# Attention and mixture-of-experts kernel: a third expert slot is multiplied by seven products of halves

## Chip, cores and metric

One core of a Trainium2 chip runs the whole kernel in one launch. The metric is the device time of an execution in microseconds; three executions of the kernel before gave 539.89, 539.95 and 541.04 us.

## What is computed

```python
# attention over 32 memories; batch 8, heads 8, seq 576, head_dim 64
a = softmax(phi, axis=memories)
k_m = einsum('bhsm,bhsd->bhmd', a, k); v_m = einsum('bhsm,bhsd->bhmd', a, v)
attn = softmax(q @ k_m^T / 8) @ v_m
x = attn.transpose(0, 2, 1, 3).reshape(4608, 512)
# mixture of 8 experts, one for each token
logits = x @ w_gate                       # 4608 x 8
e_idx = argmax(logits, axis=1)
gate_w = softmax(logits)[e_idx]
eom = sigmoid(x @ w_output_gate)
for e in range(8):
    h  = relu(x[e_idx == e] @ w1[e])      # 512 -> 1024
    out[e_idx == e] = gate_w * eom[:, e] * (h @ w2[e])   # 1024 -> 512
```

## The kernel before

The program has two parts that overlap. The first computes attention and writes x to a DRAM buffer `xs`, two batches ("pair") at a time; VectorE (DVE) then ranks the tokens by expert (`rank`) and derives lists of token rows, an early list from the first two pairs (`route_early`) and a late one when all four are through (`route_late`). A list is made by `table`: DVE compares (line 232, tile `eql`), TensorE (PE) adds up 144 small products (line 242, PSUM tile `pr`), DVE writes the indices.

The second part runs eight big **slots** of 576 tokens of one expert each, slots 0 to 3 from the early list and 4 to 7 from the late one (with these inputs no smaller slot is used after them). For a slot GpSimd (POOL) gathers the rows of x (`gathers`, line 441), they are transposed and cut into a high and a low part (`xh`, `xl`, `turn_x`), and each weight block of 128x1024 (`w`, fetched by SyncE, line 495) is cut likewise by `Stream.split`: ScalarE (ACT) casts the high part (line 537), DVE subtracts for the low one (line 542), into a ring of buffers `whl`. Every product is three matmuls: high by high, low by high, high by low. The first layer gives `hh` and `hl` (lines 1276 and 1281), the second `y` (line 1442), which is scaled and scattered by POOL (line 1267). `nine` emits a slot; its second layer also prepares the next slot's x.

The first layer exists in two forms. `plain` (slots 0, 1, 2, in `WHOLE`) transposes x on PE (lines 1136, 1141) and multiplies whole: 16 banks (PSUM tiles of 288 columns) of 12 matmuls, 192 in all (line 1310). `seven` (slots 3 to 7, in `SEVEN`) splits both operands in halves and forms seven products P1 to P7 of 4 x 6 matmuls, 168 in all (line 1338). It needs sums of weight quarters (S1 to S4, `Stream.prep`: DVE lines 511, 517, 519, POOL line 515), sums of x quarters (T1 to T4, DVE line 1120) and x transposed by DVE instead of PE: `relay` moves squares of 32 rows by 16 DMAs on SyncE's queue (line 457, tile `xq`), line 1102 transposes them. A `seven` slot has 11 splits, a `plain` one 8.

The order of work on each engine is the order in which the program emits it. After each bank a `hook` advances what runs beside the slots: attention by `HOOK[0]` pieces and the ranking by `HOOK[1]` pieces. `LATE` holds a piece back for so many ticks after what it needs was emitted. `SUMS6`, `EXTRA6`, `TURN6`, `GATHER` and `RELAY` say at which steps of a slot the preparation of the next one is emitted; steps 0 to 15 are its first layer, 16 to 35 its second.

Buffers come from stacked pools. `settle` (when attention is done, at the end of slot 0) closes the attention's pools, `reopen` (step 2 of slot 2) closes the ranking's, and each calls `grow(k)`, which adds `GROW[k]` buffers to the rings (`whl`, `w`, `xg`). `rebank` deals the eight PSUM banks anew: 4 for `ps`, 4 for `pc`, which the seven products accumulate in.

Of the kernel before, what the change touches and what calls it, by code (L numbers as in the profile page):

```python
# [7 lines left out]
F32 = mybir.dt.float32  # L8
# [8 lines left out]
P = 128  # L17
B, H, S, D, M = 8, 8, 576, 64, 32
NTOK, DM, E, F = 4608, 512, 8, 1024
# [8 lines left out]
SL = S  # L28
NHB = SL // 64
NCL = (NHB + 1) // 2  # L30
NPE, NPL, NSS = 4, 4, 28
# [4 lines left out]
ORDER = ["R4", "X", "S", "R0", "m", "D", "M", "B", "V0", "R1", "R1", "V1", "M", "W", "m", "C"]  # L36
LAG = {"X": 1, "B": 2, "D": 1, "V": 3, "C": -1}
TICK = 0
HOOK = (3, 2)
START = 17  # L40
SWAP = ()
NKV = 8
# [7 lines left out]
NPK = 1  # L50
PHI1 = 6
NEA = 3
LATE = {"lg": 8, "w": 2, "pe": 3, "dve": 2}
GROW = ((4, 0, 0), (2, 0, 0), (0, 2, 0))
SOON = {"pe": 3, "dve": 0, "tab": 12, "w": 3, "ix": 2}
PACE = 30
BESIDE = ((14, 15), (13, 14))
# [7 lines left out]
EXTRA6 = (1, 3, 11, 14, 17, 19)  # L65
EXTRA7 = (2, 6, 9, 12, 17, 19)
GATHER = {8: 2, 12: 2, 16: 1}
LAST = 1
OPEN = (2, 2)
WHOLE = tuple(range(NPE - 1))  # L70
SEVEN = tuple(range(NPE - 1, NPE + NPL))
PROD = ("P1", "P2", "P6", "P5", "P3", "P7", "P4")
SPLITS = {"P1": (0, 2), "P6": (2,), "P5": (0, 2)}
SUMS = {"P6": "S2", "P5": "S1", "P3": "S4", "P7": "S3"}
FREED = {"P1": 0, "P2": 0, "P6": 0, "P5": 1, "P3": 0, "P7": 2}
XQ = 144
XROW = 4 * XQ


HEADS = (0, 2, 4, 6, 1, 3, 5, 7)  # L80
# [3 lines left out]
def attention_moe(tc, phiT, kv, qT, wgo, wall, out):  # L84
    nc = tc.nc
    V, A, G, T = nc.vector, nc.scalar, nc.gpsimd, nc.tensor

    with contextlib.ExitStack() as ctx:
# [30 lines left out]
        prt = ctx.enter_context(contextlib.ExitStack())  # L119
# [265 lines left out]
        env = {}  # L385
# [36 lines left out]
        ring = Ring([P, 2, 1024], F32R, "whl")  # L422
# [24 lines left out]
        def relay(z, to=4):  # L447

            if not z["quart"]:
                return  # L450
            if "xq" not in z:
                z["xq"] = env["st"].tile([P, NCL, 4, P], F32, name="xq")
                z["a"] = 0
            for a in range(z["a"], to):
                for b in range(4):
                    m = 1 if not z["big"] else NCL if b < 2 else NCL - 1
                    nc.sync.dma_start(z["xq"][32 * a:32 * a + 32, 0:m, b],
                                      z["xg"][32 * b:32 * b + 32, 0:m, XQ * a:XQ * a + P])
                z["a"] = a + 1

# [609 lines left out]
        def turn_x(z, c):  # L1070
# [3 lines left out]
            nb, n = (NCL, SL) if big else (1, P)  # L1074
            if c == 0:
# [6 lines left out]
                m = min(nb, 4)  # L1082
# [17 lines left out]

            def square(c):
                V.transpose(z["xt"][:, c, 0:n].rearrange("p (k i) -> p k i", i=32),
                            z["xq"][:].rearrange("p k b q -> p (k b) q")[:, 0:n // 32, 32 * c:32 * c + 32])

            if z["seven"]:
                xt = z["xt"].rearrange("p a (b s) -> p a b s", b=2)

                src = {"B11": xt[:, 0:2, 0], "B21": xt[:, 2:4, 0], "B22": xt[:, 2:4, 1]}
                if c == 0:
                    for k in range(4):  # L1110
                        square(k)
                elif c == 1:
                    for nm in src:
                        A.copy(z[nm][0], src[nm])
                    tr = env["st"].tile([P, NCL, 4, P], F32, name="xq")[:].rearrange("p k b q -> p (k b q)")
                    z["r"] = r = {nm: tr[:, SL * o:SL * o + SL].rearrange("p (a s) -> p a s", a=2)
                                  for o, nm in enumerate(("T1", "T2", "T3", "T4"))}
                    for nm, x, y in (("T1", xt[:, 0:2, 1], xt[:, 0:2, 0]), ("T2", xt[:, 2:4, 1], r["T1"]),
                                     ("T3", xt[:, 2:4, 1], xt[:, 0:2, 1]), ("T4", xt[:, 2:4, 0], r["T2"])):
                        V.tensor_tensor(r[nm], x, y, ALU.subtract)  # L1120
                elif c == 2:
                    for nm, x in z["r"].items():
                        A.copy(z[nm][0], x)
                    for nm in src:
                        V.tensor_tensor(z[nm][1], src[nm], z[nm][0].bitcast(F32), ALU.subtract)
                else:
                    for nm, x in z["r"].items():
                        V.tensor_tensor(z[nm][1], x, z[nm][0].bitcast(F32), ALU.subtract)
                return
# [115 lines left out]
        mo = None  # L1245
# [9 lines left out]
        PASS = ((0, 0), (1, 0), (0, 1))  # L1255

        def finish_y(z, k, py):
            y = mo.tile([P, DM], F32, name="y", bufs=4)
            n = P
            if k == NCL - 1:  # L1260

                n = 64
                A.copy(y[0:n], py[64:128])
                V.tensor_tensor(y[0:n], py[0:n], y[0:n], ALU.add)
                py = y
            A.activation(y[0:n], py[0:n], AF.Copy, scale=z["g"][0:n, k:k + 1])  # L1266
            G.indirect_dma_start(  # L1267
                out=out, out_offset=bass.IndirectOffsetOnAxis(ap=z["idx"][1][0:n, z["q0"] + k:z["q0"] + k + 1], axis=0),
                in_=y[0:n], in_offset=None, bounds_check=NTOK - 1, oob_is_err=False)
# [47 lines left out]
        def seven(i, st, hook):  # L1317

            z, h = order[i], [hidden() for _ in range(4)]
            if "pad" not in env:  # L1320
                env["pad"] = env["st"].tile([P, 24], F32, name="pad")
            step, made = [-1, 0], [None]

            def tell(new=None):
# [89 lines left out]
        def nine(i, st, nxt, hook):  # L1414

            z = order[i]
            h = (seven if z["seven"] else plain)(i, st, hook)
            wei.finish()
            more = i + 1 < st.hi and order[i + 1]["seven"]
            if more and "pc" not in env:  # L1420
                rebank()
            turn, extra, sums = (TURN, (), {}) if not more else (
                (TURN7, EXTRA7, SUMS7) if z["seven"] else (TURN6, EXTRA6, SUMS6))
            if z["seven"]:
# [90 lines left out]
        def settle():  # L1515

            att.finish()
            pso.close()
            pa.close()
            env["rl"] = prl.enter_context(tc.tile_pool(name="rl", bufs=1, side="right", reuse_waits="tile"))  # L1520
            env["cap"] = raw.size
            grow(1)
            env["ps"] = prp.enter_context(tc.tile_pool(name="p1", bufs=7 - NPK, space=PSUM, reuse_waits="tile"))
# [2 lines left out]

        def reopen():

            late.finish()
            prl.close()  # L1530
            prt.close()
            env["st"] = ctx.enter_context(tc.tile_pool(name="st", bufs=1, side="right", reuse_waits="tile"))
            grow(2)
            env["cap"] = raw.size

        def rebank():
            prp.close()
            prr.close()
            for key, nm, n in (("ps", "p2", 4), ("pc", "pc", 4)):
                env[key] = ctx.enter_context(tc.tile_pool(name=nm, bufs=n, space=PSUM, reuse_waits="tile"))  # L1540

        def run(st):
# [8 lines left out]
            def hook(step, new):  # L1551
                if (i, step) == OPEN:
                    reopen()
                wei.step()
                if step < 16 or not drip.gens:
                    gathers(i)
                if i + 1 < hi and order[i + 1]["seven"]:
                    if step in RELAY and (gat[0] > i + 2 or gat[0] > i + 1 and not drip.gens):
                        relay(order[i + 1], 2 * RELAY.index(step) + 2)
                clock[0] += not att.gens  # L1560
                att.step(HOOK[0])
                (rou if rou.gens else late).step(HOOK[1])

# [25 lines left out]
        n = NPE + NPL  # L1589
# [52 lines left out]
```

## Time and profile before

| | |
|---|---|
| median of 3 executions | 539.95 us (539.89 to 541.04) |
| the profiled execution's own time | 543.56 us |
| its span, first to last instruction | 541.6 us |
| PE busy | 506.0 us (93%) |
| DVE busy | 375.6 us (69%) |
| ACT busy | 280.9 us (52%) |
| POOL busy | 164.8 us (30%) |
| mean granted TensorE clock | 0.964 of full speed |

The profile is of one execution. A matmul's recorded duration overlaps the next one's, so PE is read here by when a stage starts and ends, not by the sum of durations. The slots stand in it as follows (us from the span's start): slot 0 from 118.1, its second layer from 150.4; slot 1 from 183.1, second layer from 209.0; slot 2 from 240.9, second layer from 266.4; slot 3, the first of seven products, from 292.5, second layer from 314.8; slot 4 from 340.95. PE ends at 534.85.

### The profile page before, as it was taken

Reading aid. Unit: us, or ns where it says so; the run is one execution under the profiler, and the core shown is the slowest. Engines: PE = TensorE matmul, PEld = TensorE weight load, DVE = VectorE, ACT = ScalarE, POOL = GpSimd, SP = SyncE. Lnnn points to the kernel's source line nnn. Section 1 sums busy time; section 2 is a strip of 40 time slices with the busy share of each in tenths; the row PEclk is TensorE's granted clock in tenths of the full one; section 3 lists DMA queues with packets and bytes.
Section 4 is the critical chain, followed back from the end, with each engine's and each line's share of the span. In section 5 each row is a group of like instructions: output and inputs, shape, how many; then the busy total and the mean of one; then the engine's idle time right before and its main releaser. Section 6 shows DMA issues by size and latency. Waiting matters only on the chain. (4 is left out here: it accounts for less than half of the span.)

```text
span 541.6 us, 11081 instructions
## 1 busy us (share of the span) xinstructions
PE 506.0 (93%) x4205; PEld 429.5 (79%) x4205; DVE 375.6 (69%) x870; ACT 280.9 (52%) x535; POOL 164.8 (30%) x168
## 2 busy tenths in 40 slices
PE   3788886989999999999999999999999999999995
PEld 2455554769877898789988988998898899889983
DVE  4374889787942698545593898688789878978600
ACT  4475764265533453244264756665574666548311
POOL 2242554543421330214146114302621341130021
PEclk9977998599999999999999999999999999999999
DMA  8999999888353664218407832980594188130011
GB/s 317 424 392 386 413 412 398 289 308 254 128 170 110 213 224 125 88 50 322 87 12 229 268 78 72 304 209 8 178 267 133 45 292 216 36 95 34 0 50 45
DMA packets 42111, 104.01 MB, mean 192 GB/s; under 512 B 4992, under 2 KB 16576, under 8 KB 41664
## 3 DMA queue, kind: packets, MB, share of 16 engines
q1 hardware_dynamic: 36160, 83.15, 46.0%
q0 software_dynamic: 5888, 20.06, 10.8%
q8 instruction: 35, 0.57, 0.4%
q14 instruction: 28, 0.23, 0.1%
HBM read 77.23 MB, written 20.05 MB: 180 GB/s over the span
## 5 line engine op out<-in xcount | busy, mean ns | idle before, releaser
L1442 PE MATMUL bps<-whl,hh 128*128 128x512 f32 x560 | 170.4, 398 | 0.0
L542 DVE TENSOR_TENSOR whl<-w,whl 128x1024 fp32r<-128x1024 f32 x74 | 90.7, 1233 | 48.6 <-ACT whl L537 40.2
L1442 PEld LDWEIGHTS bps<-whl,hh 128*128 128x128 f32 x560 | 104.7, 188 | 24.7
L1442 PE MATMUL bps<-whl,hl 128*128 128x512 f32 x216 | 85.4, 395 | 0.0
L537 ACT CAST whl<-w 128x1024 fp32r<-128x1024 f32 x74 | 76.8, 1049 | 4.3 <-PE bpc L1442 2.8
L1310 PE MATMUL bps<-xh,whl 128*128 128x288 f32 x384 | 77.6, 298 | 0.0
L1310 PEld LDWEIGHTS bps<-xh,whl 128*128 128x128 f32 x384 | 61.5, 188 | 1.3 <-DVE gr L1061 0.4
L1267 POOL DMA_INDIRECT out<-y,idx_oa x20 | 26.0, 1300 | 105.3 <-ACT y L1266 80.9
L1310 PE MATMUL bps<-xl,whl 128*128 128x288 f32 x192 | 54.8, 296 | 0.0
L1267 POOL DMA_INDIRECT out<-y,idx_ol x20 | 22.7, 1137 | 104.0 <-ACT y L1266 70.5
L1338 PE MATMUL bpc<-xh,whl 128*128 128x288 f32 x240 | 49.4, 296 | 0.0
L1338 PE MATMUL bpc<-th,whl 128*128 128x288 f32 x240 | 49.3, 295 | 0.0
L1442 PEld LDWEIGHTS bps<-whl,hl 128*128 128x128 f32 x216 | 40.7, 188 | 9.3
L1266 ACT ACTIVATE y<-bps,gx 128x512 f32<-128x512 f32 x27 | 18.6, 689 | 44.7 <-PE bps L1442 39.8
L1276 ACT ACTIVATE hh<-bps 128x288 fp32r<-128x288 f32 x48 | 19.7, 411 | 39.9 <-PE bps L1310 38.8
L1338 PEld LDWEIGHTS bpc<-xh,whl 128*128 128x128 f32 x240 | 38.9, 188 | 0.2
L1338 PEld LDWEIGHTS bpc<-th,whl 128*128 128x128 f32 x240 | 39.0, 188 | 0.0
L1276 ACT ACTIVATE hh<-keep 128x288 fp32r<-128x288 f32 x60 | 26.7, 445 | 22.7 <-DVE keep L1349 22.7
L901 ACT COPY xo<-bpd 128x576 f32<-128x576 f32 x36 | 22.2, 641 | 28.1 <-issue 9.5
L1310 PEld LDWEIGHTS bps<-xl,whl 128*128 128x128 f32 x192 | 35.6, 188 | 0.2
L857 POOL TENSOR_TENSOR ea<-ea,mx 128x512 f32<-128x512 f32 (+1 forms) x18 | 17.6, 977 | 59.5 <-DVE mx L855 51.3
L1338 PE MATMUL bpc<-tl,whl 128*128 128x288 f32 x120 | 35.4, 295 | 0.0
(246 smaller groups left out, 950.3 us busy)
## 6 DMA issues: line engine op xcount, KB each, us to landing
w<-wall SPq DMA_DIRECT2D x64, 512.0 KB
kvt<-kv SPq DMA_DIRECT2D x32, 512.0 KB
xs<-xo SPq DMA_DIRECT2D x16, 576.0 KB
qt<-qT SPq DMA_DIRECT2D x16, 512.0 KB
ph<-phiT SPq DMA_DIRECT2D x3, 1152.0 KB
xq<-xg SPq DMA_DIRECT2D x40, 80.0 KB
xq<-xg SPq DMA_DIRECT2D x40, 64.0 KB
kv<-kv SPq DMA_DIRECT2D x4, 512.0 KB
```

The source lines that it names most:

```text
L537: A.copy(hl[:, 0], w[:])
L542: V.tensor_tensor(hl[:, 1], w[:], hl[:, 0].bitcast(F32), ALU.subtract)
L857: (V if z["k"] in BESIDE[0] else G).tensor_tensor(eav, eav, mx[:, 0:n].unsqueeze(2).to_broadcast([P, n, M]), ALU.subtract)
L901: A.copy(xo[:, c % 2], px[:, :, 0:2 * XQ])
L1266: A.activation(y[0:n], py[0:n], AF.Copy, scale=z["g"][0:n, k:k + 1])
L1267: G.indirect_dma_start(out=out, out_offset=bass.IndirectOffsetOnAxis(ap=z["idx"][1][0:n, z["q0"] + k:z["q0"] + k + 1], axis=0), in_=y[0:n] ...
L1276: A.activation(h_[:, j, c:e], src, AF.Relu)
L1310: T.matmul(pb, w[:, b, o:o + P], x[a][:, cc, c * SL // 2:(c + 1) * SL // 2], start=(n == 0), stop=(n == 11))
L1338: T.matmul(pb, w[:, b, o:o + P], z[x][a][:, kc], start=(first and n == 0), stop=(n == 5), skip_group_check=not first)
L1442: T.matmul(py, a, w[:, b, DM * f:DM * f + DM], start=(u == 4 and f == 0 and n == 0), stop=(u == 7 and f == 1 and n == len(ps) - 1))
```

## The change

Slot 2 leaves `WHOLE` and joins `SEVEN`. The pool `st`, which holds `xq`, the sums and the kept products, is opened in `settle` rather than in `reopen`, and the ranking's pool `rt` is kept to the end; `xq` loses 2 of 20 blocks, a pad goes, `y` has 3 buffers rather than 4. The rings grow in another order: 6, then 7, then 8 buffers for `whl` (before 6, 8, 8), 5, 6, 7 for `w` (before 5, 5, 7). `rebank` stands at the start of slot 2 rather than before slot 2's second layer. Attention and ranking advance by 4 and 3 pieces a hook rather than 3 and 2, the ranking's PE work is held back 5 ticks rather than 3, and one more split is emitted at step 12 of slot 2 (`MORE`).

```diff
-HOOK = (3, 2)
+HOOK = (4, 3)
-LATE = {"lg": 8, "w": 2, "pe": 3, "dve": 2}
-GROW = ((4, 0, 0), (2, 0, 0), (0, 2, 0))
+LATE = {"lg": 8, "w": 2, "pe": 5, "dve": 2}
+GROW = ((4, 0, 0), (1, 1, 0), (1, 1, 0))
-LAST = 1
+LAST = 0
 OPEN = (2, 2)
-WHOLE = tuple(range(NPE - 1))
-SEVEN = tuple(range(NPE - 1, NPE + NPL))
+MORE = (2, 12)
+WHOLE = tuple(range(NPE - 2))
+SEVEN = tuple(range(NPE - 2, NPE + NPL))
...
-                z["xq"] = env["st"].tile([P, NCL, 4, P], F32, name="xq")
+                z["xq"] = env["st"].tile([P, NXQ, P], F32, name="xq")
...
-                    nc.sync.dma_start(z["xq"][32 * a:32 * a + 32, 0:m, b],
+                    nc.sync.dma_start(z["xq"][32 * a:32 * a + 32, b:4 * m - 3 + b:4],
...
-            y = mo.tile([P, DM], F32, name="y", bufs=4)
+            y = mo.tile([P, DM], F32, name="y", bufs=3)
...
             z = order[i]
+            if z["seven"] and "pc" not in env:
+                late.finish()
+                rebank()
             h = (seven if z["seven"] else plain)(i, st, hook)
             wei.finish()
             more = i + 1 < st.hi and order[i + 1]["seven"]
-            if more and "pc" not in env:
-                rebank()
...
             pa.close()
+            env["st"] = ctx.enter_context(tc.tile_pool(name="st", bufs=1, side="right", reuse_waits="tile"))
...
         def reopen():
-            late.finish()
             prl.close()
-            prt.close()
-            env["st"] = ctx.enter_context(tc.tile_pool(name="st", bufs=1, side="right", reuse_waits="tile"))
             grow(2)
...
             def hook(step, new):
                 if (i, step) == OPEN:
                     reopen()
+                if (i, step) == MORE:
+                    st.split(ring.size, wait=True)
```

In the built program slot 2's 192 matmuls of line 1310 and its 20 transposes are gone and 168 matmuls of line 1338 stand in their place. Lines of the changed kernel are one or two higher than those before (542 is 544, 232 is 234, 1310 is 1312, 1338 stays). Three places in the order of the engines follow.

DVE, before, where the late list is compared: all of it stands in slot 1's second layer, since the row above it finishes a `y`.

```order
L1264 TENSOR_TENSOR y<-bps,y 64x512
L371 TENSOR_TENSOR q_3069<-q_3069,q_3066 128x36
L373 TENSOR_TENSOR q_3063<-q_3063,q_3069 128x36
L215 TENSOR_TENSOR tm<-ohg,tb 128x288
L219 TENSOR_REDUCE q_3104<-tm 128x36
L376 TENSOR_TENSOR q_3104<-jg,q_3104 128x36
L378 TENSOR_TENSOR q_3063<-q_3063,q_3104 128x36
L232 TENSOR_TENSOR eql<-iota_bl,q_3063 128x864 x4
L542 TENSOR_TENSOR whl<-w,whl 128x1024
```

And in the change:

```order
L544 TENSOR_TENSOR whl<-w,whl 128x1024
L1283 SCALAR_TENSOR_TENSOR hl<-bps,hh 128x288
L378 TENSOR_TENSOR q_2940<-jg,q_2940 128x36
L380 TENSOR_TENSOR q_2889<-q_2889,q_2940 128x36
L234 TENSOR_TENSOR eql<-iota_bl,q_2889 128x864
L1283 SCALAR_TENSOR_TENSOR hl<-bps,hh 128x224
L1283 SCALAR_TENSOR_TENSOR hh<-bps,hh 128x64
L234 TENSOR_TENSOR eql<-iota_bl,q_2889 128x864 x3
L1283 SCALAR_TENSOR_TENSOR hl<-bps,hh 128x288
L1283 SCALAR_TENSOR_TENSOR hl<-bps,hh 128x224
L1283 SCALAR_TENSOR_TENSOR hh<-bps,hh 128x64
L544 TENSOR_TENSOR whl<-w,whl 128x1024
```

The comparisons moved up into slot 1's first layer, among the remainders of its banks 8 to 11 of 16 (two halves 288 and 224 + 64 a pair of banks).

PE, before, from the end of the list's 144 products into slot 1's second layer:

```order
L242 LDWEIGHTS Aw
L242 MATMUL pr<-eql,Aw 64x48
L1442 MATMUL bps<-whl,hh 128x512
L1442 MATMUL bps<-whl,hl 128x512
L1442 MATMUL bps<-whl,hh 128x512 x2
L1442 MATMUL bps<-whl,hl 128x512
L1442 MATMUL bps<-whl,hh 128x512
L1136 MATMUL bps<-ident,xg 128x128 x4
L1141 MATMUL bps<-ident,xg 128x64 x4
L1442 MATMUL bps<-whl,hh 128x512
```

And in the change:

```order
L244 LDWEIGHTS Aw
L244 MATMUL pr<-eql,Aw 64x48
L1443 MATMUL bps<-whl,hh 128x512 x17
L1443 MATMUL bps<-whl,hl 128x512
L1443 MATMUL bps<-whl,hh 128x512 x2
L1443 MATMUL bps<-whl,hl 128x512
```

The list's products moved from within the second layer to its very front (the 17 matmuls begin with the 16 of its first row block), and the transposes no longer follow.

SyncE's queue, before, at the fetch of slot 2's weights during slot 1's first layer:

```order
L493 TENSOR_LOAD slot
L493 ISA x2
L495 ISA
L495 DMA w<-wall 128x1024
L495 ISA
L495 DMA w<-wall 128x1024
L495 ISA
L495 DMA w<-wall 128x1024
L495 ISA
L495 DMA w<-wall 128x1024
L495 ISA
L495 DMA w<-wall 128x1024
```

And in the change:

```order
L497 ISA
L497 DMA w<-wall 128x1024
L459 DMA xq<-xg 32x5x128 x2
L459 DMA xq<-xg 32x4x128 x2
L459 DMA xq<-xg 32x5x128 x2
L459 DMA xq<-xg 32x4x128 x2
L497 ISA
L497 DMA w<-wall 128x1024
L459 DMA xq<-xg 32x5x128 x2
L459 DMA xq<-xg 32x4x128 x2
L459 DMA xq<-xg 32x5x128 x2
L459 DMA xq<-xg 32x4x128 x2
```

Sixteen moves for slot 2 now stand in two halves round the fetch of its fifth weight block; the four blocks that its sums need are ahead of them.

## Rows read from the trace of the kernel before

**Rows 1.** The page: PE's busy tenths in 40 equal slices of the span.

```profile
PE   3788886989999999999999999999999999999995
```

**Rows 2.** Windows by stage, slots 0 to 3: stretch, then each engine's busy us.

```profile
core 0: us, PE busy (x) PEld busy (x) DVE busy (x) ACT busy (x) POOL busy (x), PEclk, DMA share, GB/s
118.10:150.40 32.30, 31.93 (x302) 29.31 (x300) 27.01 (x68) 16.29 (x31) 14.29 (x12) 1.00 0.60 191
150.40:183.10 32.70, 32.70 (x181) 25.17 (x181) 13.01 (x32) 13.60 (x21) 4.77 (x6) 1.00 0.42 139
183.10:209.00 25.90, 25.90 (x205) 25.81 (x204) 21.92 (x84) 12.44 (x24) 8.97 (x8) 1.00 0.68 224
209.00:240.90 31.90, 31.39 (x278) 25.47 (x277) 17.99 (x42) 10.17 (x15) 4.00 (x4) 1.00 0.21 63
240.90:266.40 25.50, 25.50 (x194) 25.48 (x193) 14.11 (x37) 10.74 (x22) 7.35 (x6) 1.00 0.69 221
266.40:292.50 26.10, 26.10 (x114) 21.06 (x113) 19.03 (x27) 10.73 (x16) 14.72 (x9) 1.00 0.32 83
292.50:314.80 22.30, 22.30 (x170) 22.26 (x169) 17.88 (x48) 16.45 (x36) 4.11 (x4) 1.00 0.85 250
```

**Rows 3.** Timeline of PE in slot 1's second layer: start, us, what.

```profile
224.01 1.91 PE L242 MATMUL pr<-eql,Aw 128*64 128x48 bf16 x94
...
227.30 0.50 PE L1442 MATMUL bps<-whl,hh 128*128 128x512 f32 x1
...
228.80 0.60 PE L1136 MATMUL bps<-ident,xg 128*128 128x128 f32 x4
...
237.70 0.60 PE L1136 MATMUL bps<-ident,xg 128*128 128x128 f32 x4
```

**Rows 4.** Windows of DVE alone: sum of three (191.05 to 196.68), then two more.

```profile
sum 2.43, DVE 2.40; mean DVE 0.80
...
210.05:210.56 0.51, 0.48 (x3) 1.00 0.00 0
211.70:221.35 9.65, 9.41 (x26) 1.00 0.26 68
```

**Rows 5.** Groups of DVE in slot 2's first layer: count, busy us, mean ns.

```profile
L542 DVE TENSOR_TENSOR whl<-w,whl 128x1024 fp32r<-128x1024 f32 x6 | 7.3, 1225 | 2.1 <-ACT whl L537 2.1
L1281 DVE SCALAR_TENSOR_TENSOR hl<-bps,hh 128x288 fp32r<-128x288 f32 x8 | 3.6, 454 | 3.5 <-ACT hh L1276 2.7 <-issue 0.8
L1281 DVE SCALAR_TENSOR_TENSOR hl<-bps,hh 128x224 fp32r<-128x224 f32 x7 | 2.7, 392 | 5.6 <-ACT hh L1276 4.4 <-issue 1.0
L1281 DVE SCALAR_TENSOR_TENSOR hh<-bps,hh 128x64 fp32r<-128x64 f32 x7 | 1.5, 215 | 0.0
```

**Rows 6.** Timeline of DVE and POOL: the same pairs beside each other, and apart.

```profile
146.29 3.30 DVE L542 TENSOR_TENSOR whl<-w,whl 128x1024 fp32r<-128x1024 f32 x2
191.66 2.35 DVE L542 TENSOR_TENSOR whl<-w,whl 128x1024 fp32r<-128x1024 f32 x2
...
146.31 4.30 POOL L955 TENSOR_TENSOR Aw<-ow,tok_hl 128x576 bf16<-128x576 bf16 x2
...
196.42 2.46 POOL L955 TENSOR_TENSOR Aw<-ow,tok_hl 128x576 bf16<-128x576 bf16 x2 [4.06 <-DVE ti L318]
```

**Rows 7.** Timelines in slot 2: DVE's preparation of slot 3, SyncE's moves, ACT's last y.

```profile
267.48 1.22 DVE L511 TENSOR_TENSOR w<-w 128x1024 f32<-128x1024 f32 x1
...
283.78 1.22 DVE L542 TENSOR_TENSOR whl<-w,whl 128x1024 fp32r<-128x1024 f32 x1
...
257.25 10.44 SPq L457 DMA_DIRECT2D xq<-xg  x16
...
292.78 0.69 ACT L1266 ACTIVATE y<-bps,gx 128x512 f32<-128x512 f32 x1 [3.21 <-PE bps L1442]
```

**Rows 8.** Who PE waited for: total us, times, longest; the ranking in slot 0.

```profile
PE pr L967 <- DVE ohg L927: 0.4, 1, 0.4
```

More of the change, by code (lines that the diff above doesn't have):

```diff
@@ L77 @@
 XROW = 4 * XQ
+NXQ = SL // 32
 HEADS = (0, 2, 4, 6, 1, 3, 5, 7)
@@ L1102, in square @@
                 V.transpose(z["xt"][:, c, 0:n].rearrange("p (k i) -> p k i", i=32),
-                            z["xq"][:].rearrange("p k b q -> p (k b) q")[:, 0:n // 32, 32 * c:32 * c + 32])
+                            z["xq"][:, 0:n // 32, 32 * c:32 * c + 32])
             if z["seven"]:
@@ L1114, in turn_x @@
                         A.copy(z[nm][0], src[nm])
-                    tr = env["st"].tile([P, NCL, 4, P], F32, name="xq")[:].rearrange("p k b q -> p (k b q)")
+                    tr = env["st"].tile([P, NXQ, P], F32, name="xq")[:].rearrange("p k q -> p (k q)")
                     z["r"] = r = {nm: tr[:, SL * o:SL * o + SL].rearrange("p (a s) -> p a s", a=2)
@@ L1319, in seven @@
             z, h = order[i], [hidden() for _ in range(4)]
-            if "pad" not in env:
-                env["pad"] = env["st"].tile([P, 24], F32, name="pad")
             step, made = [-1, 0], [None]
```

## The prediction

> **What bounds the kernel now.** I read the page's slices first: up to about a fifth of the span PE's digit varies, after that it is 9 in every slice but the last [rows 1]. So from slot 0 on the time is PE's, and a stage is priced by how long PE takes to get through it, which the windows by stage show: PE is busy for the whole of nearly every stretch, at a granted clock of 1.00, the upper of its two levels, 2.4 GHz [rows 2]. No other engine is full there: DVE has 27.0 of 32.3 us in slot 0's first layer, 21.9 of 25.9 in slot 1's and 19.0 of 26.1 in slot 2's second, ACT less. What the change saves on PE it saves in the end, unless DVE, which it loads more, becomes late.
>
> **The part on PE.** Slot 2's first layer took 25.5 us for 192 matmuls; slot 3's, the same work as seven products, took 22.3 us for 168 [rows 2], both 133 ns a matmul. Slot 2 in the new form should take what slot 3 took: **3.2 us less**.
>
> Slot 2's x is no longer transposed on PE. Those 20 transposes lie in slot 1's second layer, from 228.80 on, in four groups [rows 3]. Adding up overlapping records is unsafe, so I subtract: that layer took 31.9 us, slot 2's, which holds the same 112 matmuls and no transposes or list, took 26.1 [rows 2]. Of the 5.8 between them the list's products are 3.3, from 224.01 to 227.30, where the layer's own matmuls resume [rows 3]. That leaves **2.5 us** for the transposes and the refilling after each. The records alone give 0.6 a group [rows 3], 2.4 for four, which agrees.
>
> The list's 144 products and the ranking's 22 are only moved along PE's queue, to other places between full stretches: nothing. PE's one wait for the ranking in slot 0, 0.4 us [rows 8], may go, because the products stand further behind what they need; I count 0 and keep −0.4 for the range.
>
> Together 3.2 + 2.5 = 5.7 us.
>
> **What pays for it.** (1) *The list in slot 1.* The products of the list now stand at the front of slot 1's second layer, so PE waits there if DVE has not finished the comparisons. The old trace does not show that wait, so I bound it by DVE's work in slot 1's first layer. It was 21.9 us busy. Out of the stretch go three pieces of the ranking's head, 2.4 us together; into it come 0.5 and 9.4 us, of which about 0.6 is the finishing of a y that stays behind [rows 4]: 21.9 − 2.4 + 9.3 = 28.8 us of work for 25.5 us. DVE is overfull in that layer. But what stands in its queue behind the last comparison doesn't count: one weight remainder of 1.23 us and three pairs of hidden remainders at 0.45 + 0.39 + 0.22 = 1.06 us [rows 5], 4.4 us by durations. That leaves 24.4 us against 25.5. On the other side, part of the 4.0 us in which DVE was idle in that stretch before are gaps between small dependent operations, which no fuller queue closes. So the list is ready between 1.1 us early and 2.9 us late. The nearer row is the early end, since most of that idle time was waiting for ACT (the remainders of hidden banks show 7.1 us of that in slot 2 [rows 5]) and that goes when DVE runs behind. I take a **wait of 0.5 us** and keep 0 to 3.
>
> While DVE runs behind, PE can also run out of banks: it may be six banks ahead of the remainders. By the work counted, DVE is at most 3 us behind before the comparisons end, two banks of 1.6 us. Nothing.
>
> (2) *Slot 0.* Attention advances 4 pieces a bank, not 3. DVE had 27.0 of 32.3 us in the first layer and 13.0 of 32.7 in the second [rows 2]; of the 13.0, three weight remainders are 3.7, and if half of the other 9.3 came forward the first layer would hold 31.7 of 32.3. It still fits: 0, with 0 to 1.5 for the range. No PE work is added, so what was last in the second layer is only earlier.
>
> (3) *Preparing slot 2.* Three more weight blocks to split, the sums S and T, the transposes on DVE and the lows of x were done for slot 3 in slot 2's second layer. The chain on DVE ran there from 267.48 to 285.0, **17.5 us** [rows 7], beside PE. In slot 1 it starts when DVE is through with the remainders, some 4 us into the second layer by (1), and ends some 22 us into a layer that, with the list in front, is 29.4 us long: 7 us of cover. The 16 moves took SyncE 10.4 us [rows 7], in which it waited for the gathered rows; in the change they stand in slot 1's first layer, ahead of everything that needs them by the layer's rest, and the four weight blocks for the sums are fetched before them. DMA was 0.68 and 0.21 busy in slot 1 [rows 2]. Nothing on the path; without that cover each us of lateness costs one.
>
> (4) *Banks.* They are dealt anew at slot 2's start, where PE passes at once from y's banks to the four `pc` banks. ACT finishes the last y 0.9 us after the next slot has begun (292.78 + 0.69 against 292.5 [rows 7, 2]). Only if the first bank is the one that held it would PE wait, 0.9 us; the built program lets the first three banks wait for ACT one after another, so the last y falls rather to the third, which PE reaches 1.6 us in. I take 0, bounds 0 and 0.9.
>
> (5) *Buffers.* Seven `whl` rather than eight in slot 1 and three y rather than four put some splits and one write further back. Slot 2's fourth product is split after most of slot 1 instead of a few steps earlier, still 10 us ahead of its use. 0, up to 2 if ACT is held up.
>
> **Sum:** 5.7 − 0.5 = 5.2 us. The profiled execution's 541.6 us of span would become 536.4, its own time of 543.56 us 538.4. The median of the runs is 3.6 us below that time; I take the difference over: 539.95 − 5.2 = **534.7 us**.
>
> **Rivals.** *DVE late in slots 0 and 1.* For it: 28.8 us of work in a 25.5 us layer. Against: 4.4 of that stands behind what PE waits for. It decides from a wait of 1.5 us; with 1.5 to 4 us the time is 535.8 to 538.3. What could add to it is POOL. When its two products for the ranking ran beside two weight remainders, DVE took 3.30 us for what takes it 2.35 alone, and POOL 4.30 instead of 2.46 [rows 6]; the change puts that pair beside DVE's fullest stretch, at slot 1's start. By these rows one such meeting costs DVE 0.95 us, the wait becomes about 1.4 and the time 535.7; were DVE held for all of POOL's 2.46 us, the wait would be 3.0 and the time 537.2. The Trainium skill, in "SBUF — State Buffer", section "Who interferes with whom", says that a DVE instruction with two SBUF inputs contends with a GpSimd instruction that reads SBUF, and that the one that comes second is blocked for the whole of the other. By that rule the second case is the one to expect; the trace agrees that both lose, but DVE by 0.95 us, less than a half of POOL's pair.
>
> *Slot 2 starves.* Fewer buffers put its later splits behind PE: a cast and a remainder late would be some 2 us, 1 to 3 with the bank of (4): 535.3 to 537.3. Against it: slot 3 went through the same with splits only a few steps earlier and PE was busy for all of its 22.3 us [rows 2].
>
> *DVE becomes the bound of slot 1, and the kernel gets slower.* In slot 1 DVE would have 28.8 and then about 19.0 us (the row of the layer that prepared slot 3 [rows 2]), 47.8 us, while PE takes 25.5 + 3.3 + 26.1 = 54.9. It decides when gaps in DVE's queue exceed 7 us; slots 1 and 2 had 4.0 and 7.1 us of them in the corresponding stretches [rows 2], 11 in all, mostly waits for ACT and PE. If all stayed, slot 2 would begin 4 us late. To be slower by over 0.2% it takes 5.7 + 1.1 more than the 7, 14 us of gaps or a weight sum that waits that long for its blocks: at least 541.1 us.
>
> **How the numbers follow.** 0.2% of the time, 1.1 us, is about what a measurement of this kernel can tell from no change. The forecast (a list's wait up to 1.5, perhaps the 0.4 gained) has 0.62 and would give 533.8 to 535.8. DVE late has 0.20, half of it by POOL; slot 2 starving 0.11; DVE as the bound 0.07, of which 0.05 slower. The range is 533.8 to 537.6: it leaves out the rest of the first rival beyond a wait of 3.4 us, the third rival and a larger gain than counted, 0.18 together. Faster by over 0.2% means below 538.9: the forecast, the second rival and most of the first, 0.88; within it, 0.07, the rest of the third rival and the case that the first two come together; slower, 0.05.
>
> **What would show it.** The windows by stage: slot 2's first layer near 22.3 us, slot 1's second near 29.4 plus any wait; PE's waits listing the list's products behind DVE's comparisons at about 0.5 us; no wait of PE at slot 2's start above 1 us; DVE near full in slot 1's first layer. I am wrong if PE shows gaps in slot 0, if the list's products wait more than 2 us, or if slot 2's products wait for weight sums or for moves.

## The result, and the profile after

The changed kernel takes **535.81 us** (median of 4 runs, 535.13 to 537.03) where the kernel before took 540.5 beside it: a ratio of 0.9915, 95% interval 0.989 to 0.9941. The interval is a gain of 3.2 to 5.9 us; the medians differ by 4.7. The forecast was 534.7 in a range of 533.8 to 537.6. The profiled execution took 537.03 us, its span 535.2, 6.4 us less than before.

The page after, busy time of each engine:

```profile
span 535.2 us, 11075 instructions
...
PE 497.1 (93%) x4161; PEld 423.0 (79%) x4161; DVE 394.1 (74%) x898; ACT 290.4 (54%) x552; POOL 167.2 (31%) x170
...
PE   3778876889999999999999999999999999999994
```

PE is busy 8.9 us less, DVE 18.5 us more, and PE's digits after the first fifth are still all 9 but the last [rows 1]: PE is still the bound.

The windows by stage after, slots 0 to 3 with a first and a second layer each (slot 1's second begins with the list; columns as in [rows 2]):

```profile
117.65:151.19 33.54, 33.54 (x318) 30.36 (x317) 29.59 (x75) 18.41 (x35) 14.79 (x13) 1.00 0.57 188
151.19:182.56 31.37, 31.37 (x177) 24.50 (x176) 13.23 (x43) 12.10 (x18) 5.82 (x6) 1.00 0.45 144
182.56:208.14 25.58, 25.58 (x193) 25.41 (x191) 24.99 (x83) 11.60 (x23) 7.74 (x7) 1.00 0.68 209
208.14:237.54 29.40, 28.68 (x258) 23.52 (x257) 22.22 (x38) 10.74 (x16) 14.33 (x10) 1.00 0.36 91
237.54:259.80 22.26, 22.26 (x169) 22.26 (x168) 17.67 (x45) 16.54 (x35) 3.35 (x3) 1.00 0.90 259
259.80:286.03 26.23, 26.23 (x115) 21.09 (x113) 23.77 (x36) 14.32 (x21) 9.42 (x8) 1.00 0.32 87
286.03:308.27 22.24, 22.24 (x169) 22.24 (x168) 17.88 (x48) 16.45 (x36) 5.62 (x5) 1.00 0.93 283
308.27:334.38 26.11, 26.11 (x114) 21.08 (x113) 22.36 (x31) 13.55 (x19) 10.65 (x9) 1.00 0.28 76
```

Set against [rows 2], stage by stage: slot 2's first layer went from 25.5 to 22.3 us, slot 1's second with the list from 31.9 to 29.4. Slot 0 moved 1.2 us from its second layer to its first and is 0.1 shorter in all; slot 1's first layer lost the 0.3 us of ranking products that now lie in slot 0. All else is within 0.2. From slot 0's start to PE's end the time fell from 416.77 to 410.47 us, 6.3 us. The stretch ahead of slot 0 varies from run to run, 115.7 to 119.8 us in the profiles of this study, so the experiments below are compared from slot 0's start on. Slot 0 itself takes 64.9 to 65.7 us in nine profiles whose program is the same up to there, so a difference of less than 1 us in it shows nothing by itself. The timed ratios are known only to 1 to 3 us either way; the sizes of the terms below are read from the traces, one profiled execution of each kernel.

The timelines of DVE and PE round the list in the changed kernel (start, us, what, idle time before it):

```profile
205.87 2.02 DVE L234 TENSOR_TENSOR eql<-iota_bl,q 128x864 bf16<-128x864 bf16 x2
207.80 0.75 DVE L1283 SCALAR_TENSOR_TENSOR hl<-bps,hh 128x288 fp32r<-128x288 f32 x2
...
208.14 2.46 PE L244 MATMUL pr<-eql,Aw 128*64 128x48 bf16 x143
211.32 0.18 PE L244 MATMUL pr<-eql,Aw 128*64 128x48 bf16 x1 [0.72 <-issue]
211.43 0.96 PE L1443 MATMUL bps<-whl,hh 128*128 128x512 f32 x3
```

The last comparison ends at 207.88, PE comes to the list at 208.14: ready 0.26 us early, no wait for DVE (the 0.72 us before the last product is listed behind nothing). DVE is busy for 24.99 of that layer's 25.58 us, so the layer is as full as forecast. The list takes 3.29 us, as before [rows 3].

### The profile page after: what moved, and what is told of

Read it like the earlier page. It is cut to its first block, busy times and chain, and to the rows that moved or that the text cites. A ratio compares the mean times of both kernels' runs of the same rounds, so it can differ in the third digit from the quotient of the medians.

```text
span 535.2 us, 11075 instructions
## 1 busy us (share of the span) xinstructions
PE 497.1 (93%) x4161; PEld 423.0 (79%) x4161; DVE 394.1 (74%) x898; ACT 290.4 (54%) x552; POOL 167.2 (31%) x170
## 4 chain that ended last, share of the span: by engine, by line
PE 71%; DMA 12%; issue 7%; DVE 5%; ACT 3%; SPq 1%; POOLq 0%; POOL 0%; ACTq 0%
PE bps L1443 29%; PE bpc L1338 18%; PE bps L1312 10%; PE bpc L1443 5%; DMA xs<-xo 5%; DMA kvt<-kv 4%; DMA out<-y,idx_ol 3%; PE bps L1338 3%; PE bpd L901 2%; ACT xo L903 1%; PE bps L1138 1%; PE bpd L840 1%; ACT ph L681 1%; DVE ea L850 1%; PE pk L734 1%
## 5 line engine op out<-in xcount | busy, mean ns | idle before, releaser
L1338 PE MATMUL bpc<-xh,whl 128*128 128x288 f32 x288 | 59.2, 296 | 0.0
L1338 PE MATMUL bpc<-th,whl 128*128 128x288 f32 x288 | 59.1, 295 | 0.0
L1312 PE MATMUL bps<-xh,whl 128*128 128x288 f32 x256 | 52.1, 299 | 0.0
L1338 PEld LDWEIGHTS bpc<-xh,whl 128*128 128x128 f32 x288 | 46.6, 188 | 0.3
L1338 PEld LDWEIGHTS bpc<-th,whl 128*128 128x128 f32 x288 | 46.7, 188 | 0.0
L1338 PE MATMUL bpc<-tl,whl 128*128 128x288 f32 x144 | 42.4, 294 | 0.0
L1312 PEld LDWEIGHTS bps<-xh,whl 128*128 128x128 f32 x256 | 40.9, 188 | 1.6 <-issue 0.6
L1338 PE MATMUL bpc<-xl,whl 128*128 128x288 f32 x144 | 42.2, 293 | 0.0
L517 POOL TENSOR_TENSOR s<-w 128x512 f32<-128x512 f32 x12 | 15.2, 1288 | 75.5 <-issue 41.3
L903 ACT COPY xo<-bpd 128x576 f32<-128x576 f32 x36 | 22.2, 642 | 26.3 <-issue 10.6
L1312 PE MATMUL bps<-xl,whl 128*128 128x288 f32 x128 | 35.9, 296 | 0.0
```

The lines of the kernel that those rows point to most:

```text
L517: G.tensor_tensor(s2[:, o], a22[:, o], a21[:, o], ALU.subtract)
L903: A.copy(xo[:, c % 2], px[:, :, 0:2 * XQ])
L1312: T.matmul(pb, w[:, b, o:o + P], x[a][:, cc, c * SL // 2:(c + 1) * SL // 2], start=(n == 0), stop=(n == 11))
L1338: T.matmul(pb, w[:, b, o:o + P], z[x][a][:, kc], start=(first and n == 0), stop=(n == 5), skip_group_check=not first)
```

## The experiments

Each kernel was timed against the kernel before on the same chip; ratios are to that one, and the changed kernel's own is 0.9915.

**The two terms of the gain.** First the transposes, put back as dead work (they transpose a constant into banks that nobody reads) where the kernel before had them.

```diff
+        def dead(z, c):
+            pt = bank([512], "ps")
+            for k in range(4):
+                T.transpose(pt[:, k * P:(k + 1) * P], ident[:], ident[:])
...
+                if i == 1 and step in TURN:
+                    dead(order[i], TURN.index(step))
```

> The changed kernel with 20 transposes of the identity put back where slot 2's transposes stood in slot 1's second layer, into banks that nobody reads. Theory (the transposes and the refilling after each cost 2.5 us of PE): slot 1's second layer takes 31.9 us again rather than 29.4, the kernel near 538.3 us. Rival (that part of the gain came from elsewhere, from what ACT and DVE no longer do for them): under 1.2 us.

Measured: 539.25 us, ratio 0.9939 (0.992 to 0.9958). Slot 1's second layer without the list takes 29.46 us against 26.11, 3.35 more, and 0.83 of that is a wait at its end, which PE lists at slot 2's start (the layer's window, and PE's wait):

```profile
210.39:239.85 29.46, 28.63 (x134) 22.90 (x133) 18.74 (x28) 10.13 (x16) 15.21 (x10) 1.00 0.36 98
...
PE bpc L1347 <- ACT y L1277: 0.8, 1, 0.8
```

PE waits there for ACT to evict a y. That the five extra banks turn the rotation so that slot 2's first `pc` bank is the one that held slot 1's last y is read from the program, not from the trace; it is the upper bound of step (4). What is left, 2.5 us, is the transposes' price as forecast.

Then the products: slot 2's x is moved and transposed by DVE as in the change, but no sums are formed and the multiplication is whole. The whole products take x in the arrangement made for halves, so slot 2's values differ; the amount of work does not.

```diff
-SEVEN = tuple(range(NPE - 2, NPE + NPL))
+SEVEN = tuple(range(NPE - 1, NPE + NPL))
...
-                if i + 1 < hi and order[i + 1]["seven"]:
+                if i + 1 < hi and order[i + 1]["quart"]:
```

> The changed kernel, slot 2 with its x moved and transposed on DVE as in the change, but multiplied whole: 192 matmuls instead of 168, no sums. It multiplies x in the arrangement made for halves, so slot 2's values differ from the reference's. Theory: the products alone are 3.2 us: slot 2's first layer takes 25.5 us again, slot 1's second stays near 29.4, the time is 539.0. Rival: the seven products pay more than they show in their own layer (their sums load DVE and POOL in slot 1, their splits run on into slot 2's second layer): then slot 1 or slot 2's second layer gets shorter by 0.5 us or more without them, and the time is 538.5 or less.

Measured: 541.64 us, ratio 0.9964 (0.9944 to 0.9985). Slot 1's list and second layer, then slot 2's first layer:

```profile
208.73:237.79 29.06, 28.68 (x258) 23.52 (x257) 14.33 (x28) 9.96 (x14) 3.92 (x4) 1.00 0.39 119
237.79:263.27 25.48, 25.48 (x193) 25.48 (x192) 15.27 (x38) 11.66 (x24) 7.37 (x6) 1.00 0.71 222
```

The first layer takes 25.48 us, 3.22 more. The list and second layer take 29.06 against 29.40, though DVE has 14.3 us of work there instead of 22.2, and the difference is in the list, whose length varies from 2.7 to 3.6 us between profiles in which it does not wait. Slot 2's second layer takes 26.3 us against 26.2 when its wait of 0.83 us is taken off. So the sums cost PE nothing that can be seen, against the rival. The banks are dealt a slot later here, and again the first `pc` bank waits for the last y, 0.83 us, at slot 3's start.

**How near the list is to a wait.** All four comparisons of the late list were done twice, or (with `nm == "l" and c == 0` as the condition) only the first.

```diff
-                V.tensor_tensor(eq[:, c:c + w], iota_blk[nm][:].unsqueeze(1).to_broadcast(b3),
-                                q[:, c:c + w].unsqueeze(2).to_broadcast(b3), ALU.is_equal)
+                for _ in range(1 + (nm == "l")):
+                    V.tensor_tensor(eq[:, c:c + w], iota_blk[nm][:].unsqueeze(1).to_broadcast(b3),
+                                    q[:, c:c + w].unsqueeze(2).to_broadcast(b3), ALU.is_equal)
```

> The changed kernel with one comparison of the late list written twice, 0.98 us more on DVE. Theory (0.26 us of slack): a wait of 0.7 us at the list, slot 1's second layer 0.7 us longer. Rival (slack of a microsecond or more): no wait.

Measured, one doubled: 536.29 us, ratio 0.9881 (0.9832 to 0.993); list and second layer 29.46 us, no wait. The rival held.

> The changed kernel with each of the four comparisons of the late list written twice, 3.9 us more on DVE in slot 1's first layer. Theory (DVE is full there and the list was ready only 0.26 us before PE came to it): PE waits about 3.7 us for the comparisons and the kernel is about 3.7 us slower than the changed one, near 539.4 us. Rival (the list has slack, or DVE's lateness is absorbed by banks and buffers): no wait above 1 us, time unchanged at 535.8.

Measured, all doubled: 538.85 us, ratio 0.995 (0.9927 to 0.9972). PE's timeline, and two windows, the list and the 5.6 us behind it:

```profile
206.55 1.32 PE L245 MATMUL pr<-eql,Aw 128*64 128x48 bf16 x72
208.31 0.75 PE L245 MATMUL pr<-eql,Aw 128*64 128x48 bf16 x36 [0.44 <-DVE eql L235]
210.37 0.75 PE L245 MATMUL pr<-eql,Aw 128*64 128x48 bf16 x36 [1.31 <-DVE eql L235]
```

```profile
206.55:211.05 4.50, 2.75 (x145) 2.53 (x144) 4.43 (x8) 1.34 (x2) 0.00 (x0) 1.00 0.73 122
211.05:216.66 5.61, 5.61 (x22) 4.44 (x18) 5.52 (x14) 0.03 (x1) 0.00 (x0) 0.70 0.18 69
```

The products come in quarters of 36, each of which needs one comparison, so PE begins with what is there: 3.9 us more on DVE make 1.75 us of waits, not the 3.7 of the theory. But the list and the layer are 32.17 us, 2.8 longer: behind the waits the granted clock is 0.70, and the rest of the layer takes 1.56 us more than the 26.11 us it had. So a late DVE is a real danger here, with about 1 us to spare: 0.98 us more cost nothing, 3.9 cost 2.8.

**The pace of attention and ranking.** Alone, then taken back.

```diff
-HOOK = (3, 2)
+HOOK = (4, 3)
```

> The kernel before, with attention and ranking at the changed pace (4 and 3 pieces a hook rather than 3 and 2) and nothing else. Theory: the pace only moves work along PE's queue and alone gives nothing: 540 us, within 1 us of the kernel before; the list's 144 products stand in slot 1's first layer, slot 1 as a whole stays 57.8 us (25.9 + 31.9), slot 2's first layer stays 25.5. Rival: part of the gain is the pace's own (PE's 0.4 us wait for the ranking in slot 0 goes, the list leaves a layer that also holds transposes): 1 us or more faster from slot 0's start to slot 2's.

Measured, the kernel before with this line: 544.2 us, ratio 1.0025 (0.9997 to 1.0052). From slot 0's start to slot 2's it takes 124.9 us, before 122.8. Slot 1 is 57.65 us, as before. Slot 0 is 2.2 us longer, and PE's waits in its first layer are these:

```profile
PE pr L967 <- DVE ohg L927: 1.4, 1, 1.4
...
PE bpd L838 <- ACT xo L901: 0.5, 1, 0.5
```

The first is the ranking's, which PE now meets too soon: 1.0 us more than before [rows 8]. A wait like the second, 0.6 us, stands also in the profile of the seven-buffer kernel below, whose slot 0 is that of the changed one, so it can't be put down to the pace. The rest of the 2.2 us is not accounted for. The timed ratio cannot be told from no change; the rival, 1 us or more faster, fell, and by the trace the pace alone costs about 1 us. What takes the first wait back is the ranking's longer hold of 5 ticks:

```diff
-LATE = {"lg": 8, "w": 2, "pe": 5, "dve": 2}
+LATE = {"lg": 8, "w": 2, "pe": 3, "dve": 2}
```

> The changed kernel with the ranking's PE work held back 3 ticks, as before, not 5: the list's products then stand before the last 48 matmuls of slot 1's first layer, which PE reaches 6.4 us sooner, while DVE's comparisons keep their place. Theory: PE waits about 6 us for DVE, which nothing gives back, and the kernel is near 541.8 us, no faster than the one before the change. Rival (DVE's order adapts, or PE's wait only moves work that DVE was late with anyway): a wait under 2 us, time within 1 us of 535.8.

Measured, the changed kernel with 3 ticks: 538.7 us, ratio 0.9934 (0.9909 to 0.996). My expectation of a 6 us wait at the list fell: DVE's comparisons come earlier along with the products they hang on, three waits of 0.22 us, and slot 1 takes 55.29 us against 54.98. The cost is in slot 0, 66.21 against 64.91 us (64.9 to 65.7 with the hold of 5), with the first wait of above, which the changed kernel does not have:

```profile
PE pr L969 <- DVE ohg L929: 1.2, 1, 1.2
...
PE pr L244 <- DVE eql L234: 0.7, 3, 0.2
```

And the changed kernel at the old pace:

```diff
-HOOK = (4, 3)
+HOOK = (3, 2)
```

> The changed kernel with the old pace of 3 and 2 pieces a hook. The late list's comparisons (9.4 us of DVE with what belongs to them) then fall into slot 1's second layer, where the changed kernel has 22.2 us of DVE's work in 29.4 us for preparing slot 2. Theory: 22.2 + 9.4 = 31.6 us of work does not fit into 29.4, so the preparation of slot 2 ends late, PE waits at the start of slot 2 or in its first layer for sums, transposed x or weight parts, 2 to 5 us: 538 to 541 us. Rival: what prepares slot 2 stands ahead of the comparisons in DVE's queue, and what falls behind is needed only later: under 0.7 us of waits, 535.5 to 536.5 us.

Measured: 544.64 us, ratio 1.0023 (0.9995 to 1.005): the whole gain is gone. From slot 0's start to slot 2's it takes 126.68 us, the changed kernel 119.89; slot 1's second layer with the list alone is 36.20 against 29.40. PE's timeline there:

```profile
230.91 0.75 PE L244 MATMUL pr<-eql,Aw 128*64 128x48 bf16 x36 [0.77 <-DVE eql L234]
231.88 0.96 PE L244 MATMUL pr<-eql,Aw 128*64 128x48 bf16 x36 [0.21 <-DVE eql L234]
236.66 2.13 PE L244 MATMUL pr<-eql,Aw 128*64 128x48 bf16 x72 [3.82 <-DVE eql L234]
238.71 0.80 PE L1443 MATMUL bps<-whl,hh 128*128 128x512 f32 x1
```

The mechanism was right (comparisons and preparation in one layer are too much for DVE), but the place was not, and the size was above the 2 to 5 us expected: the preparation stands ahead in DVE's queue, so PE waits 4.8 us at the list, not at slot 2; the other 2 us are again a lower clock, 0.75 in the list and 0.79 behind it, from 238.71 to 245.73. So the pace earns nothing by itself, but the change stands on it: it puts the comparisons a layer ahead of the preparation.

**The buffers.** The ring of weight parts ends at 7 instead of 8; and, in another kernel, the extra split of slot 2 is left out.

```diff
-GROW = ((4, 0, 0), (1, 1, 0), (1, 1, 0))
+GROW = ((4, 0, 0), (1, 1, 0), (0, 1, 0))
```

> The changed kernel, whose ring of low weight parts stays at 7 buffers to the end instead of growing to 8 in slot 2. Theory of step (5), buffers cost nothing: a buffer fewer only puts splits a few steps further back, each still some 10 us ahead of its use; 535.8 us, every slot from slot 2 on within 0.2 us. Rival: the seven products, with 11 splits to a slot, live on the eighth buffer: each of slots 3 to 7 waits for a split, 0.5 to 2 us a slot, 538 to 545 us.

```diff
-MORE = (2, 12)
+MORE = (2, 99)
```

> The changed kernel without the extra split at step 12 of slot 2. Theory: the split comes a few steps later and is still early enough, 535.8 us relative to the changed kernel, slot 2's two layers within 0.2 us of 22.3 and 26.2. Rival: slot 2's second layer or slot 3 waits for a weight part, 1 to 2 us.

Measured: 539.15 us, ratio 0.9919 (0.9887 to 0.9951), and 540.39 us, ratio 0.9954 (0.9933 to 0.9975). The ratio of the first can't be told from the changed kernel's, the traces of both can. Slot 3's second layer, windows of the one and of the other kernel:

```profile
309.05:335.71 26.66, 26.43 (x114) 21.00 (x113) 22.61 (x31) 13.43 (x19) 10.91 (x10) 1.00 0.38 102
```

```profile
309.18:335.74 26.56, 26.29 (x115) 20.98 (x114) 22.45 (x31) 13.31 (x19) 11.11 (x9) 1.00 0.37 98
```

and PE's timeline in the first:

```profile
316.70 1.21 PE L1443 MATMUL bps<-whl,hh 128*128 128x512 f32 x4 [0.23 <-DVE whl L544]
```

Both take 0.5 us more than the changed kernel's 26.11, with one wait for a split. In slots 4 to 6 the second layer is 26.6 to 26.7 us long as well, in the changed kernel 26.0 to 26.2. Without the extra split, slot 2's second layer is 0.5 us longer too (26.71 us). The theory fell in both: a buffer fewer, or one split not sent ahead in slot 2, costs some 0.5 us a slot up to slot 6, 2.2 and 2.6 us in all from slot 2's start on. For the ring that is the low end of the rival; for the split the rival had 1 to 2 us in one layer, and it came as 0.5 in each of five. That the splits stay a step behind from slot to slot is what the repeated wait suggests; their order was not followed through.

**How much cover slot 2's preparation has.** Six (`range(6)`), then sixteen of its transpositions on DVE were done again (0.69 us each).

```diff
                     for k in range(4):
                         square(k)
+                    if z is order[2]:
+                        for k in range(16):
+                            square(k % 4)
```

> The changed kernel with six of slot 2's transpositions on DVE (0.69 us each) done a second time, 4.1 us more in slot 1's second layer, in the middle of the preparation. In the changed kernel that preparation ends at 229.3, 8.2 us before slot 2 begins at 237.5. Theory of step (3), 7 us of cover: nothing, 535.8 us relative to the changed kernel, slot 2 begins 29.4 us after the list. Rival: the parts of x are needed earlier than slot 2's start, or what ACT and POOL make of them follows late: PE waits 1 us or more at slot 2's start or in its first layer.

Measured: 536.98 us, ratio 0.9876 (0.984 to 0.9913): nothing lost in four of five runs (535.8 to 537.2). The fifth, the profiled one, took 542.53, and shows 3.0 us of the wait that follows. By their times the theory held in four executions and the rival in one: this kernel stands at the edge.

> The changed kernel with sixteen of slot 2's transpositions done again, 11.0 us more on DVE, 2.8 us beyond the 8.2 us of cover. Theory of step (3), beyond its cover each us of lateness costs one: PE waits 2.8 us at slot 2's start or in its first layer, 538.6 us. Rival: the last pieces in DVE's queue are the parts of T and the last weight sum, of which the first of the seven products need none, so PE goes on and the products absorb it: a wait of at most 0.7 us.

Measured: 547.84 us, ratio 1.0079 (1.0053 to 1.0105), slower than the kernel before. The profiled execution, at 544.74 us, is the fastest of the ten. PE waits 7.6 us at slot 2's start, and for neither x, T nor sums, but for ACT to evict slot 1's last y. PE's wait, and ACT's timeline:

```profile
PE bpc L1341 <- ACT y L1271: 7.6, 1, 7.6
```

```profile
227.19 0.72 ACT L1271 ACTIVATE y<-y,gx 64x512 f32<-64x512 f32 x1 [13.08 <-DVE y L1269]
...
231.06 1.82 ACT L1128 CAST th<-xq 128x576 fp32r<-128x576 f32 x3
232.90 1.84 ACT L1271 ACTIVATE y<-bps,gx 128x512 f32<-128x512 f32 x3
...
244.19 0.69 ACT L1271 ACTIVATE y<-bps,gx 128x512 f32<-128x512 f32 x1 [8.51 <-DMA out<-y,idx_oa]
```

The first y waits 13 us for a DVE step that stands behind the transpositions, three more y stand behind ACT's casts of x and T, and the last waits 8.5 us for a scatter to give back one of three y buffers, POOL issuing it late because the y came late. Until then the bank is not free. A fourth y buffer tests that (for the room, one weight part fewer):

```diff
-            y = mo.tile([P, DM], F32, name="y", bufs=3)
+            y = mo.tile([P, DM], F32, name="y", bufs=4)
...
-GROW = ((4, 0, 0), (1, 1, 0), (1, 1, 0))
+GROW = ((4, 0, 0), (0, 1, 0), (1, 1, 0))
```

> The kernel with sixteen extra transpositions once more, with four y buffers again instead of three (for the room, the ring of low weight parts stays at 6 buffers in slot 1 and 7 from slot 2 on). Theory: what made PE wait 7.6 us at slot 2's start was not the late preparation itself but the last y of slot 1, whose buffer was free only when a scatter had landed; with a fourth buffer the last y is evicted at once, the wait falls to 1 us or less, and the time to that of the changed kernel plus at most 2 us. Rival: the preparation, which ends 3.4 us after slot 2's start, is late for the products as well: a wait of 2.8 us or more stays, then listed behind DVE.

Measured: 552.65 us, ratio 1.0172 (1.0105 to 1.0239). At slot 2's start there is no wait at all and its first layer takes 22.25 us, so the late preparation itself cost that layer's products nothing. The last y no longer waits for a scatter, which agrees with the buffer as the cause; the smaller ring that came with it is not tested apart. But the time got worse: in slot 2's second layer PE waits 10 us, until 17 us into it. PE's wait, and the window of that layer:

```profile
PE bps L1446 <- DVE whl L544: 10.0, 1, 10.0
```

```profile
261.83:300.72 38.89, 28.92 (x114) 22.89 (x113) 24.00 (x36) 14.28 (x21) 12.03 (x11) 0.82 0.59 173
```

The timelines of POOL, ACT and DVE there:

```profile
236.91 7.14 POOL L1272 DMA_INDIRECT out<-y,idx_oa  x1 [3.49 <-ACT y L1271]
244.36 2.39 POOL L443 DMA_INDIRECT xg<-xs,idx_ga  x1 [0.31 <-issue]
...
264.22 1.03 ACT L539 CAST whl<-w 128x1024 fp32r<-128x1024 f32 x1
...
275.29 2.75 DVE L1104 STREAM_TRANSPOSE xg<-xq 128x576 f32<-128x576 f32 x4 [3.92 <-DMA xq<-xg]
277.97 1.18 DVE L544 TENSOR_TENSOR whl<-w,whl 128x1024 fp32r<-128x1024 f32 x1
```

POOL's scatters of the late y hold up slot 3's gathers, from 230.5 in the changed kernel to 244.4 here (slot 2 begins at 237.5 and 239.6). SyncE's moves follow, then DVE's transpositions, and behind those in DVE's queue stands the low part of the weights that slot 2's second layer needs; ACT had cast its high part 13 us before. In the changed kernel the split behind these transpositions ends 9.0 us into the layer, here 17.3. The gathers were as late with three y buffers (4.8 us behind slot 2's start in both), but there PE came to the second layer 9.4 us later. How much of the 10 us the smaller ring added was not separated. No kernel of the study beat the changed one by more than its interval.

## Why the prediction was right, and where it was not

- **PE's terms.** 3.2 and 2.5 us were forecast, 3.22 and 2.52 are in the stages, and each was put back by itself at 3.22 and 2.5. The sum of 5.7 was right because both were read as differences of stages of equal content and not from added records.
- **The list, step (1).** Forecast 0.5 us of wait within 0 to 3; there is none. The work was counted right (24.4 us ahead of PE's arrival against a layer of 25.5), and the near bound was the true one: DVE has no gaps left. It is steadier than the step had it, since PE needs the comparisons in quarters. Of the 1.1 us by which the time from slot 0's start to PE's end fell further than forecast (6.3 for 5.2) it is 0.5; another 0.4 fell in slot 0 and slot 1's first layer, where PE's wait for the ranking [rows 8] is gone, which I had kept for the range; the rest, 0.2 us, is spread over the other stages.
- **Slot 0, step (2).** First layer 33.5 us with 29.6 of DVE, second 31.4: the sum stayed. But that depended on the hold of 5 ticks, which the step did not price: without it PE waits 1.2 us for the ranking there, and slot 0 is 0.5 to 1.3 us longer.
- **Preparing slot 2, step (3).** DVE's chain runs from 212.9 to 229.3, 16.4 us (17.5 forecast), 8.2 us ahead of slot 2. That reading of the cover, and "each us of lateness costs one", is the step that failed when tested: 4.1 us more cost nothing or 5.5, and 11 us cost 9.4, from slot 0's start to PE's end. The cover is not DVE's end against slot 2's start but what stands behind the chain in ACT's and POOL's queues: y, then scatters, then the next slot's gathers. The forecast did not need it, since nothing was late: its zero here was right without this reading being so.
- **Banks, step (4).** No wait here; the 0.83 us of the bound appeared in both kernels that changed how many banks are dealt ahead of the first `pc` bank.
- **Buffers, step (5).** Zero for the change as it is, but not for the reason given. The eighth weight buffer holds 2.2 us, the extra split 2.6, and three y are enough only as long as y is on time. The rival of a starving slot 2 was priced without the list's 0.5 us: with it, its 535.3 to 537.3 would have been 535.7 to 537.7.
- **DVE as the bound.** DVE's work in slot 1 is 47.2 us, 47.8 were counted. Of its gaps, 0.6 us lie in the first layer and 7.2 in the second, where most come after the preparation is done and cost nothing.
- **From the profiled time to the median.** The difference of 3.6 us between them, which the forecast took over from before, is 1.2 us after the change. The profiled time came out 1.4 us below its forecast of 538.4, the median 1.1 us above its 534.7: two errors that partly cancel, so that the number came out this close is in part luck.
- **POOL beside DVE.** The pair of POOL met two small steps of the ranking, one of which took 0.22 us and the other 1.18, and one split, which took 1.59 us for its 1.22 [rows 7]:

```profile
180.68 1.32 DVE L184 TENSOR_TENSOR pt<-ti,upto 128x64 f32<-128x64 f32 x2
L184 DVE TENSOR_TENSOR pt<-ti,upto x2: 218/698/1178, 180.7 to 180.8; 128x64 f32<-128x64 f32 x2
...
182.52 1.59 DVE L544 TENSOR_TENSOR whl<-w,whl 128x1024 fp32r<-128x1024 f32 x1
...
180.70 2.33 POOL L957 TENSOR_TENSOR Aw<-ow,tok_hl 128x576 bf16<-128x576 bf16 x2 [2.40 <-DVE ti L320]
```

It lies at the end of slot 0, in a layer where DVE has 18 us to spare, and not in slot 1's full layer as the rival feared. The prediction read [rows 6] by pairs. Single instructions of the same meeting, before the change (shortest, median, longest in ns), show more:

```profile
L542 DVE TENSOR_TENSOR whl<-w,whl x2: 1212/1690/2169, 146.3 to 147.4; 128x1024 fp32r<-128x1024 f32 x2
L955 POOL TENSOR_TENSOR Aw<-ow,tok_hl x2: 2132/2171/2210, 146.3 to 148.5; 128x576 bf16<-128x576 bf16 x2
```

The first DVE instruction took what it takes alone. Each of the three that came after it began while one of the other engine ran, and took some 1 us longer, about what the other had left (POOL's takes 1.15 us alone). The rule of the Trainium skill, "SBUF — State Buffer", "Who interferes with whom", that the second is blocked for the whole of the other, agrees with this when it is read by instruction: its price here is one POOL instruction for each DVE instruction that comes second, 0.95 us in these rows, and not the pair's 2.46 that the prediction drew from it. What it would have cost in slot 1's layer no run here shows.

## What to carry over

Price a saving by subtracting stages of equal content, and test each term by putting that piece alone back. When work is moved to a fuller engine, read the cover from every in-order queue that waits for it (here evictions, scatters and the next gathers behind DVE's chain), not from when the chain itself ends. A setting that earns nothing alone, here the pace, may be what the saving stands on, and small ones, here a hold and one split sent ahead, may each hold a part of it.

## What had not been expected of the hardware

A wait of PE can cost more than its length. These are windows of the profiled run with six extra transpositions, the wait itself and what follows:

```profile
238.63:241.62 2.99, 0.00 (x1) 0.00 (x0) 0.00 (x0) 0.74 (x2) 2.38 (x3) 0.86 0.91 325
241.62:245.00 3.38, 3.38 (x14) 3.38 (x15) 2.46 (x5) 3.38 (x6) 2.43 (x3) 0.50 0.84 229
245.00:248.00 3.00, 3.00 (x16) 3.00 (x16) 2.21 (x7) 1.27 (x5) 0.00 (x0) 0.56 0.83 239
248.00:265.08 17.08, 17.08 (x131) 17.08 (x130) 13.36 (x36) 11.22 (x24) 2.16 (x2) 1.00 0.98 261
```

The granted clock is 0.50, the level of 1.2 GHz, and then 0.56 in the mean, for some 6 us in all behind a wait of 2.99 us, and slot 2's first layer takes 28.20 us for 22.26: 3.0 of wait and 2.95 of slower products. The waits of 1.75 us (list) and 4.8 us (list at the old pace) cost 1.6 and 2 us more in this way, the single waits of 7.6 and 10 us 1.8 and 2.7 us; behind the waits of 0.83 us at a slot's start the layers took what they take otherwise, within 0.1 us. So what is added does not grow in step with the wait, and a wait's price is to be read from the length of the stage, not from the list of waits.
